# Float64 weights put together by two merges on VectorE, a ScalarE fence in every unit, and a new instruction order, in a fused RWKV attention and channel-mix kernel

## The chip, the cores and the metric

One Trainium2 chip, one of its cores. The metric is the device time of one execution in microseconds (us); several runs of the same kernel are taken and their median is compared.

## What is computed

```python
for t in range(S):                       # S = 768, batch 4, 8 heads, head_dim 48
    kt, vt, rt = k[:, :, t], v[:, :, t], r[:, :, t]
    cur = einsum('bhd,bhe->bhde', u[None] * kt, vt)
    y[:, :, t] = einsum('bhd,bhde->bhe', rt, state + cur)
    state = w[None, :, :, None] * state + einsum('bhd,bhe->bhde', kt, vt)
x = y.transpose(0, 2, 1, 3).reshape(B, S, 384)
x_prev = concatenate([zeros((B, 1, D)), x[:, :-1]], axis=1)
xk = mu_k * x + (1 - mu_k) * x_prev;  xr = mu_r * x + (1 - mu_r) * x_prev
k = maximum(xk @ w_k, 0)                 # w_k 384 x 1024
out = sigmoid(xr @ w_r) * (k * k @ w_v)  # w_r 384 x 384, w_v 1024 x 384
```

The arrays come as float64 where the weights `w_k`, `w_r`, `w_v` are concerned; the kernel gets their 64-bit words and must make float32 numbers of them itself.

## The kernel before, in words

**Attention in units.** The 768 steps are cut into 12 chunks of 64 and the 4 batches into 2 pairs: 24 units. For a unit `u`, `RK{u}` (VectorE) scales the loaded `r` and `k` by decay tables, `Kn{u}` scales `k` for the state, `ru{u}` makes the products for the bonus term. On TensorE, `sc{u}` and `bo{u}` form scores and bonus in PSUM, `Am{u}` (VectorE, two instructions) masks them, `st{u}` multiplies the old state (`from_state`, L565), `va{u}` adds the masked scores times the values (`values`, L586), `up{u}` forms the new state term (`update`, L599). ScalarE then turns the result into the tile `xt` (`tu{u}`, L624), and the state is advanced (`S{u}`; VectorE, and ScalarE for the first two units). PSUM holds one `y` and one `a` at a time, so unit `u + 1` cannot begin `st` before `tu{u}` and `S{u}` have read `y`.

**Single units and blocks.** Units 0 to 4 are single tasks. From unit 5 on, `st`, the scores of the next unit, `va` and `up` are one task `bl{u}`, written out by `block`. Between `from_state` and `values` the array's rows are used in another order, so something must hold `values` back until `from_state` has ended: in single units a fence (a 1x1 copy `tick` on ScalarE that waits for the last matmul of `from_state` and that the first matmul of `values` waits for), in blocks `nc.tensor.drain()`, which waits for all that TensorE has in flight.

**Channel mix in tiles.** Six tiles `m` of 128 steps (four units each), 512 columns. Six mixes per tile (`mixa` and `mixc` on ScalarE, `mixb` and `mixd` on VectorE) give high and low halves; `k{m}.0` to `k{m}.7` are the key products (9 matmuls each: high x high, high x low, low x high, three row blocks), followed on ScalarE by `relu`, `square`, `kh` and on VectorE by `kl`; `r{m}.0` to `.2` are the gates, `v{m}.o.c` the value products (72 matmuls a tile). Tile 0's mixes need the four units 0 to 3 and six small copies `gap0.*` that the SP queue issues after `tu3`.

**Weights.** Ten blocks (4 of `w_k`, 2 of `w_r`, 4 of `w_v`) are loaded as 64-bit words. For each, `shift{b}` (VectorE, L364) moves the high word into place, `rest{b}` (ScalarE, two instructions, L372 and L373) turns two bytes of each word into 16-bit numbers that hold sign and lowest bits together, `merge{b}` (VectorE, L377) joins the two, `hi{b}` (ScalarE) rounds to the high half, and the low half comes from TensorE with ScalarE (`lop`, `loc`, blocks 0 to 3) or from VectorE (`lo{b}`).

**Range test.** The weights are read again, half a block at a time (20 parts, `cw{b}`, two buffers `seen`); ScalarE takes absolute values (`size{b}`, L885), VectorE the largest and the smallest (L888). `check_range` compares them, a matmul `cnt` on TensorE sums the outcome, and a flag chooses at the end between this result and a slow step-by-step version.

**What sets the order.** Each engine runs its instructions strictly in the order in which they are emitted. `Plan.order` emits tasks in a simulated order of time from costs and the lists `ORDER`, one per engine, which cover the time up to the end of tile 0; behind them it goes by the longest tail. `i7` in the TensorE list means seven idle matmuls that keep the clock up. SP issues loads in its list's order, and one that has to wait holds all behind it.

Of the kernel before, what the change touches and what calls it, by code (L numbers as in the profile page):

```python
# [45 lines left out]
LEAST = 1.125 * 2.0 ** -15  # L46
MOST = 3.0e38
# [9 lines left out]
    "PE": """i22 pt sc0 bo0 i9 sc1 bo1 va0 up0 i7 va1 up1 sc2 bo2 i1 st2 lop0.0 va2 up2 lop0.1 i7 st3 sc3 bo3 lop1.1 lop1.0 va3 up3 sc4 bo4 i3 lop2.0  # L57
        lop2.1 st4 i4 va4 up4 lop3.0 sc5 bo5 lop3.1 k0.0.0 k0.0.1 k0.0 k0.1 k0.2 k0.3 bl5 k0.4 k0.5 k0.6 k0.7 bl6 r0.0 r0.1 v0.0.0 v0.0.1 bl7 v0.0.2
        v0.0.3 r0.2 v0.1.0 v0.1.1 v0.1.2 bl8 v0.1.3 v0.2.0 v0.2.1 v0.2.2""",
    "DVE": """tables RK0 ru0 RK1 Am0 ru1 Kn0 Kn1 ru2 RK2 shift0 Am1 merge0 RK3 Kn2 Am2 dec2 dec3 first0 shift1 ru3 Kn3 merge1 S2 shift2 RK4 Am3 merge2 S3  # L60
        shift3 Am4 merge3 mixb0.0.0 RK5 mixd0.0.0 mixb0.0.1 mixb0.0.2 mixd0.0.1 mixd0.0.2 shift4 mixb0.1.0 shift5 merge4 Am5 RK6 S4 merge5 mixd0.1.0
        kl0.0 kl0.1 mixb0.1.1 first1 mixb0.1.2 S5 lo4 kl0.2 RK7 mixd0.1.2 shift6 Am6 mixd0.1.1 kl0.3 lo5 merge6 kl0.4 shift7 kl0.5 merge7 lo6 RK8
        Am7 S6 kl0.7 kl0.6 lo7 shift8 shift9 merge8 RK9 lo8 rs8 Am8 S7 fin0.0 rs9 merge9 mixb1.0.0 mixb1.0.1 lo9 mixd1.0.0 RK10 mixb1.0.2 first2
        mixd1.0.1 Am9""",
    "ACT": """wup wn rest0 S0 tu0 hi0 S1 tu1 tick2 loc0.0 rest1 tu2 hi1 rest2 loc0.1 tick3 loc1.1 tu3 hi2 rest3 omu loc1.0 loc2.0 mixa0.0.0 tick4 hi3
        mixc0.0.0 mixa0.0.1 loc2.1 mixa0.0.2 mixc0.0.1 loc3.0 mixc0.0.2 mixa0.1.0 rest4 loc3.1 rest5 relu0.0 relu0.1 square0.0 tu4 mixa0.1.1
        mixc0.1.0 square0.1 kh0.0 kh0.1 mixa0.1.2 relu0.2 hi4 tu5 square0.2 kh0.2 mixc0.1.2 relu0.3 square0.3 rest6 relu0.4 hi5 kh0.3 mixc0.1.1
        square0.4 rest7 relu0.5 kh0.4 square0.5 kh0.5 relu0.6 hi6 tu6 relu0.7 square0.7 kh0.7 hi7 sg0.0 square0.6 kh0.6 rest8 sg0.1 tu7 rest9 hi8
        mixa1.0.0 mixa1.0.1 hi9 mixc1.0.0 tu8 mixa1.0.2 mixc1.0.1""",
# [21 lines left out]
class Plan:  # L91
# [12 lines left out]
    def add(self, name, engine, cost, call, after=(), lock=False, allocates=(), uses=(), size=0, quads=False, behind=()):  # L104

        assert name not in self.tasks, name
        self.tasks[name] = dict(name=name, engine=engine, cost=cost, call=call, after=[a for a in after if a], lock=lock,
                                allocates=list(allocates), size=size, quads=quads, behind=[b for b in behind if b], n=len(self.tasks))  # L110
# [268 lines left out]

# [746 lines left out]
```

## Time and profile before

| | |
|---|---|
| median of 3 runs | 355.42 us (354.82 to 358.03) |
| profiled execution, whole | 357.5 us |
| its span, first to last instruction | 355.7 us |
| TensorE busy | 327.5 us (92%) |
| VectorE busy | 230.9 us (65%) |
| ScalarE busy | 215.4 us (61%) |
| GpSimd busy | 90.1 us (25%) |
| mean granted TensorE clock | 0.973 |

Busy time is the time in which an engine has an instruction under way. The shares are averages over a start-up of some 50 us, a first tile and five more tiles with different limits, so they have to be read stage by stage. A granted clock of 1.00 is the 2.4 GHz level, 0.50 the 1.2 GHz level.

### The profile page before, as it was taken

What the parts mean: (1) busy time and instruction counts of PE and PEld (TensorE: products, weight loads), DVE (VectorE), ACT (ScalarE), POOL (GpSimd) and SP (SyncE); (2) the same over time, 40 slices, a digit from 0 to 9 for tenths busy, and PEclk for the clock granted to TensorE, in tenths of its full rate; (3) what the DMA queues carried; (4) which work ended last, traced back from release to release, by engine and by line L of the source; (5) the groups of instructions that cost most, each with busy time, mean ns of one, the idle gap of its engine ahead of it and who ended that gap; (6) DMA issues with size and microseconds to landing.
All of it is one profiled execution on the core that took longest, in us unless ns stands there. A gap on an engine that the chain in (4) does not pass through costs nothing. (4 is left out here: it accounts for less than half of the span.)

```text
span 355.7 us, 9895 instructions
## 1 busy us (share of the span) xinstructions
PE 327.5 (92%) x4309; PEld 255.6 (72%) x4309; DVE 230.9 (65%) x346; ACT 215.4 (61%) x327; POOL 90.1 (25%) x86
## 2 busy tenths in 40 slices
PE   8587978979979999999999999999999999999991
PEld 3355655857856778887778877878877778888880
DVE  7845575939689779885897669986766517433000
ACT  2438799999944976365771468662646827288000
POOL 2001504324337043701364403366102200000000
PEclk9878799989999999999999999999999999999998
DMA  7992076623355574616844428625321001100001
GB/s 215 331 328 64 17 229 239 218 82 120 100 135 184 165 227 134 203 55 188 247 143 127 122 76 257 210 69 142 106 95 44 15 5 49 59 2 0 29 35 36
DMA packets 17236, 45.39 MB, mean 128 GB/s; under 512 B 2528, under 2 KB 4704, under 8 KB 17184
## 3 DMA queue, kind: packets, MB, share of 16 engines
q1 hardware_dynamic: 17184, 44.66, 40.8%
q8 instruction: 36, 0.59, 0.7%
q14 instruction: 16, 0.13, 0.1%
HBM read 38.75 MB, written 4.72 MB: 122 GB/s over the span
## 5 line engine op out<-in xcount | busy, mean ns | idle before, releaser
L728 PE MATMUL v<-kh,wv 128*128 128x512 f32 x288 | 92.9, 393 | 0.7 <-ACT wv L413 0.5
L728 PEld LDWEIGHTS v<-kh,wv 128*128 128x128 f32 x288 | 54.0, 188 | 13.3 <-ACT wv L413 0.9
L728 PE MATMUL k<-xh,wk_hi 128*128 128x512 f32 x144 | 58.9, 409 | 3.9 <-ACT kr L760 3.3
L774 DVE TENSOR_TENSOR kl<-kr,kh 128x512 fp32r<-128x512 f32 x48 | 37.8, 790 | 34.6 <-ACT kh L769 34.5
L728 PE MATMUL k<-xl,wk_hi 128*128 128x512 f32 x144 | 57.8, 402 | 0.7 <-DVE xl L749 0.7
L728 PE MATMUL k<-xh,wk_lo 128*128 128x512 f32 x144 | 57.6, 400 | 0.0
L728 PE MATMUL v<-kl,wv 128*128 128x512 f32 x144 | 56.3, 391 | 0.0
L498 POOL TENSOR_TENSOR ru<-tokens,vk 128x384 f32<-128x384 f32 x16 | 20.5, 1281 | 105.3 <-DVE S L615 46.6
L760 ACT ACTIVATE kr<-k 128x512 f32<-128x512 f32 x48 | 28.7, 600 | 23.2 <-PE k L728 22.7
L742 DVE SCALAR_TENSOR_TENSOR xm<-xt,small_sb,xm 128x512 f32<-128x512 f32 x36 | 30.7, 869 | 16.8 <-ACT xm L738 16.1
L738 ACT ACTIVATE xm<-xt,omu 128x512 f32<-128x512 f32 x36 | 25.5, 724 | 21.4 <-DMA xt<-xt 16.2
L513 POOL TENSOR_TENSOR Kn<-vk,wn 128x384 f32<-128x384 f32 x18 | 24.3, 1352 | 52.5 <-DMA vk<-in_vk 27.0
L728 PEld LDWEIGHTS k<-xh,wk_hi 128*128 128x128 f32 x144 | 27.4, 190 | 12.2 <-ACT kr L760 4.2
L728 PEld LDWEIGHTS k<-xl,wk_hi 128*128 128x128 f32 x144 | 27.4, 191 | 7.2 <-DVE xl L749 1.1
L728 PEld LDWEIGHTS k<-xh,wk_lo 128*128 128x128 f32 x144 | 27.5, 191 | 6.7
L765 ACT ACTIVATE kr<-kr 128x512 f32<-128x512 f32 x48 | 30.3, 631 | 1.2
L728 PEld LDWEIGHTS v<-kl,wv 128*128 128x128 f32 x144 | 27.0, 188 | 5.4
L769 ACT CAST kh<-kr 128x512 fp32r<-128x512 f32 x48 | 29.6, 619 | 1.1
L486 DVE TENSOR_TENSOR RK<-rk,table 112x1024 f32<-112x1024 f32 x22 | 29.2, 1329 | 1.3 <-DMA rk<-in_rk 1.3
L797 DVE TENSOR_TENSOR sg<-v,sg 128x512 f32<-128x512 f32 x18 | 12.4, 686 | 25.8 <-PE v L728 21.1
L749 DVE TENSOR_TENSOR xl<-xm,xh 128x512 fp32r<-128x512 f32 x36 | 25.0, 704 | 4.7 <-ACT xh L746 4.1
L746 ACT CAST xh<-xm 128x512 fp32r<-128x512 f32 x36 | 22.3, 620 | 8.9 <-DVE xm L742 8.5
(100 smaller groups left out, 515.1 us busy)
## 6 DMA issues: line engine op xcount, KB each, us to landing
rk<-in_rk SPq DMA_DIRECT2D x22, 448.0 KB, 4.7
vk<-in_vk SPq DMA_DIRECT2D x24, 384.0 KB, 3.7
out<-sg SPq DMA_DIRECT2D x18, 256.0 KB, 2.0
raw_k<-in_wk SPq DMA_DIRECT2D x4, 768.0 KB, 11.5
raw_v<-in_wv SPq DMA_DIRECT2D x4, 768.0 KB, 7.6
tokens<-in_rt SPq DMA_DIRECT2D x16, 192.0 KB, 3.8
seen<-in_wk SPq DMA_DIRECT2D x8, 384.0 KB, 3.6
seen<-in_wv SPq DMA_DIRECT2D x8, 384.0 KB, 4.0
```

Of the source, the lines that this page charges most:

```text
L486: nc.vector.tensor_tensor(out=RK, in0=d["rk"], in1=table[:, :, :, :C], op=ALU.mult)
L498: nc.gpsimd.tensor_tensor(out=ru, in0=late["tokens"][:, u % 2], in1=d["kn"], op=ALU.mult)
L513: engine.tensor_tensor(out=Kn, in0=d["kn"], in1=wn, op=ALU.mult)
L728: nc.tensor.matmul(out=ps, lhsT=a, rhs=x, start=(first and i == 0), stop=(last and i == n - 1))
L738: nc.scalar.mul(out=xm, in_=before, mul=omu[:, j, t:t + 1])
L742: nc.vector.scalar_tensor_tensor(out=xm, in0=now, scalar=mu_sb[:, j, t:t + 1], in1=xm, op0=ALU.mult, op1=ALU.add)
L746: nc.scalar.copy(out=xh, in_=mixed[m, j, t])
L749: nc.vector.tensor_tensor(out=xl, in0=mixed.pop((m, j, t)), in1=xh.bitcast(F32), op=ALU.subtract)
L760: nc.scalar.activation(out=kr, in_=keys[m, f], func=AF.Relu)
L765: nc.scalar.activation(out=kr, in_=kr, func=AF.Square)
L769: nc.scalar.copy(out=kh, in_=keys[m, f])
L774: nc.vector.tensor_tensor(out=kl, in0=kr, in1=kh.bitcast(F32), op=ALU.subtract)
```

## The change

Three of its parts change instructions. `rest` goes: sign and lowest bits are now joined by two VectorE instructions, `w_sign` and `w_low`, each of the form that `w_merge` had. Every unit has the ScalarE fence, blocks included, in place of the drain. The range test's largest and smallest are taken by VectorE straight from the loaded words with an absolute value in the reduction; ScalarE has no part in it; its 20 parts lie in tiles 2 to 5 instead of 1 to 3, and `cnt` goes from `k3.1` to `v5.1.0`. The fourth part is the order: new `ORDER` lists, and other engines for `Kn`, `dec` and `ru` of the first units.

The lists of VectorE up to the first mix of tile 0, before and after:

```
tables RK0 ru0 RK1 Am0 ru1 Kn0 Kn1 ru2 RK2 shift0 Am1 merge0 RK3 Kn2 Am2 dec2 dec3 first0 shift1 ru3 Kn3 merge1 S2 shift2 RK4 Am3 merge2 S3 shift3 Am4 merge3 mixb0.0.0

tables RK0 ru0 Kn0 Am0 RK1 Kn1 RK2 Am1 shift0 sign0 first0 dec2 merge0 Kn2 Am2 dec3 ru3 RK3 shift1 sign1 merge1 S2 Am3 ru4 RK4 S3 shift2 sign2 merge2 Am4 mixb0.0.0
```

The list of SP from `w1` to `w5`, before and after:

```
w1 w2 rk4 vk4 w3 rk5 vk5 gap0.1.0 gap0.0.0 gap0.0.2 gap0.0.1 gap0.1.1 gap0.1.2 w4 w5

w1 w2 rk4 gap0.0.0 gap0.1.0 vk4 gap0.1.1 gap0.0.1 gap0.0.2 gap0.1.2 w3 rk5 vk5 w4 w5
```

`Kn` goes to VectorE for units 0 to 2 and 4 to 7 (before 0 to 3), `dec` for units 2, 3 and 5 to 7 (before 2 and 3), `ru` for units 0 and 3 to 5 (before 0 to 3); GpSimd has the others. The instructions:

```diff
-    def w_rest(b):
...
-        raw = raws[b].bitcast(U8)
-        to = raws[b].bitcast(I16)
-        nc.scalar.activation(out=to[:, :, 0], in_=raw[:, :, 3], func=AF.Identity, scale=1.0 / 32, bias=below[:, 0:1])
-        nc.scalar.activation(out=to[:, :, 1], in_=raw[:, :, 7], func=AF.Identity, scale=-2.0, bias=below[:, 1:2])
-
-    def w_merge(b):
-        a = af[b]
-        nc.vector.scalar_tensor_tensor(out=a, in0=raws[b][:, :, 0], scalar=0x80000007, in1=a,
-                                       op0=ALU.bitwise_and, op1=ALU.bitwise_or)
...
-        add(f"rest{b}", "ACT", 0.1 + 1.3 * n, lambda b=b: w_rest(b), [f"w{b}"], behind=[f"rest{b - 1}" if b else None])
-        add(f"merge{b}", "DVE", 0.07 + 0.8 * n, lambda b=b: w_merge(b), [f"shift{b}", f"rest{b}"], lock=True, uses=[f"raw{b}"])
+        add(f"sign{b}", "DVE", 0.07 + 0.8 * n, lambda b=b: w_sign(b), [f"shift{b}"], lock=True)
+        add(f"merge{b}", "DVE", 0.07 + 0.8 * n, lambda b=b: w_low(b), [f"sign{b}"], lock=True, uses=[f"raw{b}"])
...
-        d["tick"] = nc.scalar.copy(out=tick, in_=ones[:1]) if single(u) else nc.gpsimd.memset(tick, 0.0)
+        d["tick"] = nc.scalar.copy(out=tick, in_=ones[:1])
...
         from_state(u)
+        fence(u)
         if u + 1 < NU:
             scores(u + 1)
             if u + 1 < TOKENS:
                 bonus(u + 1)
-        nc.tensor.drain()
         values(u)
...
-    def sizes(b):
...
-        nc.scalar.activation(out=seen[b], in_=late["seen"][:, b % 2, :n, 1].bitcast(F32), func=AF.Abs)
...
-        nc.vector.tensor_reduce(out=bounds[:, i, b:b + 1], in_=seen[b], op=op, axis=mybir.AxisListType.X)
...
+        nc.vector.tensor_reduce(out=bounds[:, i, b:b + 1], in_=late["seen"][:, b % 2, :n, 1].bitcast(F32), op=op,
+                                axis=mybir.AxisListType.X, apply_absolute_value=True)
...
-        at = (NM - 3) * b // PARTS + 1
+        at = (NM - 2) * b // PARTS + 2
...
-    row.insert(row.index(f"k{NM // 2}.1"), "cnt")
+    row.insert(row.index(f"v{NM - 1}.1.0"), "cnt")
```

The two merges, which only the slow version called until now:

```python
    def w_sign(b):
        a = af[b]
        nc.vector.scalar_tensor_tensor(out=a, in0=raws[b][:, :, 1], scalar=0xC0000000, in1=a,
                                       op0=ALU.bitwise_and, op1=ALU.bitwise_or)

    def w_low(b):
        a = af[b]
        nc.vector.scalar_tensor_tensor(out=a, in0=raws[b][:, :, 0], scalar=29, in1=a,
                                       op0=ALU.logical_shift_right, op1=ALU.bitwise_or)
```

The planner also learns a cost for the fence (`fence=0.5` in a block).

## Rows read from the trace of the kernel before

**Rows 1.** Windows by stage: us, then busy time (instructions) by engine, PEclk, DMA share, GB/s

```profile
0.00:51.30 51.30, 40.57 (x882) 25.58 (x883) 33.32 (x53) 30.64 (x39) 8.31 (x19) 0.87 0.63 195
51.30:111.60 60.30, 53.33 (x749) 41.27 (x747) 44.85 (x63) 53.11 (x67) 22.07 (x16) 0.97 0.51 162
111.60:290.70 179.10, 176.11 (x2407) 142.15 (x2411) 134.94 (x206) 106.27 (x182) 59.71 (x52) 1.00 0.44 132
100.00:110.00 10.00, 8.61 (x156) 6.93 (x156) 9.80 (x14) 4.43 (x7) 5.20 (x5) 1.00 0.68 192
```

**Rows 2.** Timeline of TensorE: the first key product of tile 0 and of tile 1

```profile
51.27 0.39 PE L728 MATMUL k<-xh,wk_hi 128*128 128x512 f32 x1
...
111.60 0.50 PE L728 MATMUL k<-xh,wk_hi 128*128 128x512 f32 x1
```

**Rows 3.** Groups by line and shape, ScalarE: the first conversion of each kind of block

```profile
L372 ACT ACTIVATE raw_v<-raw_v,below 128x768 int16<-128x768 uint8 x4 | 8.2, 2056 | 0.0
...
L372 ACT ACTIVATE raw_k<-raw_k,below 128x768 int16<-128x768 uint8 x4 | 8.1, 2024 | 4.3 <-DMA raw_k<-in_wk 4.3
...
L372 ACT ACTIVATE raw_r<-raw_r,below 128x576 int16<-128x576 uint8 x2 | 3.2, 1610 | 0.0
```

**Rows 4.** Timeline of all engines around unit 2's end and unit 3's start

```profile
29.42 1.99 ACT L373 ACTIVATE raw_k<-raw_k,below 128x768 int16<-128x768 uint8 x1
31.17 0.68 ACT L624 COPY xt<-y 112x512 f32<-112x512 f32 x1
...
32.93 1.13 PE L565 MATMUL y<-RK,S 48*64 48x64 f32 x32 [2.36 <-DVE S L615]
```

**Rows 5.** Groups by line and shape, VectorE: the merges, and Kn where VectorE has it

```profile
L377 DVE SCALAR_TENSOR_TENSOR a_k<-raw_k,a_k 128x768 uint32<-128x768 uint32 x4 | 4.3, 1067 | 6.0 <-ACT raw_k L373 3.6 <-ACT omu L315 2.3
L377 DVE SCALAR_TENSOR_TENSOR a_v<-raw_v,a_v 128x768 uint32<-128x768 uint32 x4 | 4.0, 994 | 1.5 <-ACT raw_v L373 1.5
...
L377 DVE SCALAR_TENSOR_TENSOR a_r<-raw_r,a_r 128x576 uint32<-128x576 uint32 x2 | 1.6, 804 | 1.7 <-ACT raw_r L373 1.7
...
L513 DVE TENSOR_TENSOR Kn<-vk,wn 128x384 f32<-128x384 f32 x4 | 2.1, 550 | 0.0
```

**Rows 6.** Timeline of TensorE: the last part of unit 0's update

```profile
18.23 0.41 PE L599 MATMUL y<-vk,Kn 64*64 64x48 f32 x5 [4.64 <-issue]
```

**Rows 7.** Timeline of the SP queue: the copies gap0

```profile
41.08 4.89 SPq L635 DMA_DIRECT2D xt<-xt  x6
```

**Rows 8.** Timeline of TensorE: one block of a later tile, with its drain

```profile
121.16 0.69 PE L565 MATMUL y<-RK,S 48*64 48x64 f32 x32
121.65 0.67 PE L522 MATMUL a<-RK 48*64 48x64 f32 x32
122.45 0.68 PE L586 MATMUL y<-Am,vk 64*64 64x64 f32 x32
```

**Rows 9.** Timeline: the fences of units 2 and 4

```profile
25.24 0.69 PE L565 MATMUL y<-RK,S 48*64 48x64 f32 x32
...
26.00 0.19 ACT L574 COPY tick<-ones 1x1 f32<-1x1 f32 x1 [1.84 <-PE y L565]
...
47.00 0.17 ACT L574 COPY tick<-ones 1x1 f32<-1x1 f32 x1
...
47.23 0.54 PEld L586 LDWEIGHTS y<-Am,vk 64*64 64x64 f32 x32 [2.45 <-ACT tick L574]
```

**Rows 10.** Timeline of ScalarE: the instruction at a later block's from_state

```profile
162.21 0.60 ACT L760 ACTIVATE kr<-k 128x512 f32<-128x512 f32 x1 [3.13 <-PE k L728]
```

**Rows 11.** Range test: its reductions, its loads; then tile 5's k5.0 and v5.1.0 on TensorE

```profile
L888 DVE TENSOR_REDUCE bounds<-seen 128x1 f32<-128x384 f32 x32 | 16.0, 543 | 1.4 <-ACT seen L885 1.4
...
seen<-in_wv SPq DMA_DIRECT2D x8, 384.0 KB, 4.0
...
308.48 0.39 PE L728 MATMUL k<-xh,wk_hi 128*128 128x512 f32 x1
...
337.10 0.40 PE L728 MATMUL v<-kh,wv 128*128 128x512 f32 x1
```

More of the change, by code (lines that the diff above doesn't have):

```diff
@@ L14 @@
 I32 = mybir.dt.int32
-I16 = mybir.dt.int16
-U8 = mybir.dt.uint8
 AF = mybir.ActivationFunctionType
@@ L46 @@
 LEAST = 1.125 * 2.0 ** -15
+GREATEST = 1.75 * 2.0 ** 16
 MOST = 3.0e38
@@ L56 @@
 ORDER = {
[L57 to L69, printed above, removed]
@@ L70 @@
-    "POOL": """Kn4 ru4 dec4 ru5 Kn5 ru6 dec5 Kn6 Kn7 ru7 dec6 Kn8 ru8 Kn9 dec7 ru9 dec8 ru10""",
-    "SP": """w rk0 vk0 rk1 vk1 rk2 w0 vk2 rk3 vk3 w1 w2 rk4 vk4 w3 rk5 vk5 gap0.1.0 gap0.0.0 gap0.0.2 gap0.0.1 gap0.1.1 gap0.1.2 w4 w5 rk6 vk6 w6 w7 rk7
-        vk7 w8 w9 ut rk8 vk8 rt8 rk9 vk9 gap1.0.0 gap1.1.1 rt9 rt10 gap1.1.0 gap1.1.2 gap1.0.2 gap1.0.1 rk10 rk11 vk10 put0.0 rt11 rk12""",
+    "PE": """i22 pt sc0 bo0 i6 va0 i2 sc1 bo1 up0 sc2 bo2 va1 up1 i5 st2 i2 va2 up2 lop0.0 sc3 bo3 st3 i4 va3 up3 lop0.1 lop1.1 sc4 st4 bo4 i10 va4 i1
+        up4 lop1.0 lop2.1 k0.0.0 lop2.0 k0.0.1 k0.0 k0.1 k0.2 sc5 bo5 k0.3 lop3.0 lop3.1 k0.4 bl5 k0.5 k0.6 k0.7 bl6 r0.0 r0.1 v0.0.0 v0.0.1 v0.0.2
+        bl7 v0.0.3 r0.2 v0.1.0 v0.1.1 v0.1.2 v0.1.3 v0.2.0 bl8 v0.2.1""",
@@ new lines @@
+    "DVE": """tables RK0 ru0 Kn0 Am0 RK1 Kn1 RK2 Am1 shift0 sign0 first0 dec2 merge0 Kn2 Am2 dec3 ru3 RK3 shift1 sign1 merge1 S2 Am3 ru4 RK4 S3 shift2
+        sign2 merge2 Am4 mixb0.0.0 dec5 Kn4 mixd0.0.0 mixb0.0.1 mixb0.0.2 mixd0.0.1 mixd0.0.2 shift3 mixb0.1.0 sign3 ru5 merge3 RK5 kl0.0 shift4 Kn5
+        sign4 mixd0.1.0 kl0.1 merge4 mixb0.1.1 Am5 RK6 S4 shift5 kl0.3 lo4 Kn6 kl0.2 sign5 mixd0.1.1 dec6 shift6 mixb0.1.2 Am6 RK7 S5 kl0.4 merge5
+        sign6 mixd0.1.2 lo5 kl0.5 shift7 merge6 first1 sign7 lo6 merge7 Am7 S6 RK8 Kn7 kl0.7 kl0.6 lo7 shift8 shift9 sign8 sign9 merge8 fin0.0 rs8
+        lo8 merge9 dec7 mixb1.0.0 Am8 S7 RK9 mixb1.0.1 mixd1.0.0 lo9 mixb1.0.2""",
@@ L73 @@
+    "POOL": """ru1 ru2 dec4 Kn3 ru6 ru7 ru8 dec8 Kn8""",
+    "SP": """w rk0 vk0 rk1 vk1 rk2 w0 vk2 rk3 vk3 w1 w2 rk4 gap0.0.0 gap0.1.0 vk4 gap0.1.1 gap0.0.1 gap0.0.2 gap0.1.2 w3 rk5 vk5 w4 w5 rk6 vk6 w6 w7 rk7
+        vk7 w8 w9 ut vk8 rt8 rk8 gap1.0.2 gap1.1.1 gap1.1.0 gap1.0.0 gap1.1.2 rk9 gap1.0.1 rk10 vk9 rk11 put0.0 rt9 rt10 vk10""",
 }
@@ L102, in __init__, with add @@
         self.tasks, self.users, self.bufs = {}, defaultdict(list), {}
-    def add(self, name, engine, cost, call, after=(), lock=False, allocates=(), uses=(), size=0, quads=False, behind=()):
+    def add(self, name, engine, cost, call, after=(), lock=False, allocates=(), uses=(), size=0, quads=False, behind=(), fence=0.0):
         assert name not in self.tasks, name
         self.tasks[name] = dict(name=name, engine=engine, cost=cost, call=call, after=[a for a in after if a], lock=lock,
-                                allocates=list(allocates), size=size, quads=quads, behind=[b for b in behind if b], n=len(self.tasks))
+                                allocates=list(allocates), size=size, quads=quads, behind=[b for b in behind if b], fence=fence, n=len(self.tasks))
         for key in uses:
@@ L176, in order @@
             end = s + t["cost"]
+            if t["fence"]:
+                told = max(s + t["fence"], free["ACT"])
+                free["ACT"] = told + 0.2
+                end = max(end, told + 0.3 + t["cost"] - 2 * t["fence"])
             free[engine] = end
@@ L897, in check_range, with count @@
         n = 2 * NP + PARTS
-        nc.vector.tensor_scalar(out=ok[:, 2 * NP:n], in0=bounds[:, 0], scalar1=2.0, scalar2=None, op0=ALU.is_lt)
+        nc.vector.tensor_scalar(out=ok[:, 2 * NP:n], in0=bounds[:, 0], scalar1=GREATEST, scalar2=None, op0=ALU.is_lt)
         nc.vector.tensor_scalar(out=ok[:, n:], in0=bounds[:, 1], scalar1=LEAST, scalar2=None, op0=ALU.is_ge)
-        cnt = psM.tile([1, ok.shape[1]], F32, tag="m", name="cnt")
+        late["ok"] = ok
+    def count():
+        ok = late["ok"]
+        late["cnt"] = cnt = psM.tile([1, ok.shape[1]], F32, tag="m", name="cnt")
@@ L913, in rwkv_kernel @@
         for i, op in enumerate((ALU.max, ALU.min)):
-            add(f"{op.name}{b}", "DVE", 0.08 + 0.8 * n, lambda b=b, i=i, op=op: bound(b, i, op), [f"size{b}"], lock=True, uses=[f"ca{b}"])
-    add("range", "DVE", 1.5, check_range, [f"max{PARTS - 1}", f"min{PARTS - 1}"], allocates=[("m", "cnt")], uses=["cnt"])
+            add(f"{op.name}{b}", "DVE", 0.08 + 0.8 * n, lambda b=b, i=i, op=op: bound(b, i, op), [f"cw{b}"], uses=[f"seen{b}"])
+    add("range", "DVE", 1.5, check_range, [f"{op}{b}" for op in ("max", "min") for b in range(PARTS)])
@@ L919, in ffn @@
+    add("cnt", "PE", 0.1, count, ["range"], allocates=[("m", "cnt")])
+    add("flag", "DVE", 0.4, decide, ["cnt"], uses=["cnt"])
     def ffn(m):
```

26 lines of the change are left out of this document (13 added, 13 removed).

## The prediction

> **What bounds the kernel now.** I read the windows by stage first [rows 1], then the first key product of tile 0 and of tile 1 in TensorE's timeline [rows 2]. They cut the span into four. Up to 51.3 us no key product runs: attention units 0 to 4 and the first weights are made ready. From 51.3 to 111.6 lies tile 0, in which TensorE has something under way for 53.3 of 60.3 us. From 111.6 on TensorE is busy for 176.1 of 179.1 us in the window shown and goes on so up to about 348.3; a tail of 7.4 us (last output, flag) closes the span of 355.7. The reader is to see that the last five tiles are TensorE's own work: what is done for VectorE or ScalarE there is worth nothing, and only the drains can be taken out. What can be gained lies ahead of 111.6.
>
> There the waiting engine is mostly TensorE and the late one ScalarE: in tile 0 ScalarE is busy 53.1 of 60.3 us [rows 1]. How it holds the chain before that is seen at unit 2 [rows 4]: `tu2` comes at 31.17, right behind the second conversion of a weight block (29.42 + 1.99), and `st3` only at 32.93, released by `S2`, which waits for `tu2`. One conversion is 2.0 us long and there are two a block [rows 3]; the fence of unit 4 was late by the same kind of queue, and TensorE lost 2.45 us to it [rows 9].
>
> **The change part by part.**
>
> *Conversions off ScalarE.* The first instructions of the ten blocks take 8.1 + 3.2 + 8.2 = 19.5 us [rows 3], the second ones are as long: 39 us leave ScalarE, all ahead of 111.6. Of its 30.6 + 53.1 = 83.7 us [rows 1] some 45 stay, so it is no bound there any more. What is late next is VectorE.
>
> *A second merge on VectorE.* The new instruction has the form of the one that is there (same shape, type and stride), so its price is 4.3 + 1.6 + 4.0 = 9.9 us for ten [rows 5]. The new lists also bring VectorE `Kn4` to `Kn7` and `dec5` to `dec7` and take `Kn3` off: net six instructions of 0.55 us, 3.3 us (`dec` has no row of its own here; it is taken as `Kn`). The `ru` that VectorE has stay four. So VectorE's work up to the first key product of tile 1 rises from 33.3 + 44.9 = 78.2 us [rows 1] to about 91. That alone is a bound: 91 us without a single wait, against 111.6 now.
>
> *Start-up.* Unit 0's update stands still from 13.6 to 18.2 for nothing that the profile shows [rows 6], while the loads run; the same loads are issued ahead of it in the new order, so I let it stand. From there to the first key product are 33 us, in which the conversions of blocks 1, 2 and 3 (4 us each) lie in front of `tu2`, of the fence and low halves of unit 3, and of the fence of unit 4: 12 us. They go. In their place the second merges of blocks 0 to 2 stand in VectorE's list ahead of `S2`, `S3` and `Am4`, about 1 us each, part of it beside TensorE's own steps. I take 1 us as left: key products begin at about 40 us instead of 51.3. The copies `gap0` wait for `tu3` in both lists; they go out at 41.08 now [rows 7] and I expect them at about 31. Moved ahead of `vk4`, `w3`, `rk5` and `vk5` in the SP queue, they hold these loads back until then. `w3` serves only key products 6 and 7, and `vk4` unit 4, so I cost this at nothing; the cover is VectorE's own backlog, which reaches `Kn4` and `shift3` some 6 and 10 us after `tu3`. If that cover were gone, a load of 2 to 4 us would show.
>
> *Tile 0.* VectorE sets its end. Through 111.6 it is busy 70% of the time now, 74% within tile 0, and 98% in its fullest window, 100 to 110 [rows 1]. Walking the new list by the durations of the trace, I find waits of about 8 us besides the 91: before the tables, before `wn`, behind unit 0's standstill, and TensorE's last value products behind `lo9`. That is 99 us, a fill of 92%. Tile 1 then begins at 99 instead of 111.6: **-12.6 us**. The ends: no wait at all, 91 us, -20.6; a fill of 84%, 108 us, -3.6.
>
> *The fence for the drain.* In a later block `values` begins 1.29 us after `from_state` (121.16 to 122.45), while the scores in between begin after 0.49 [rows 8]. With the fence, from unit 2: 0.76 us to the tick (25.24 to 26.00) and 0.19 for it; unit 4 shows 0.06 more from the tick's end to TensorE (47.17 to 47.23) [rows 9]: 1.01. So a block gains 0.28 us at best. What queues behind the tick on ScalarE is the relu of the key product just ended: it starts at 162.21 now, 0.1 us after `from_state` [rows 10], and would start some 0.8 us later, which three PSUM tiles of key products cover. What may stand ahead of the tick is the rest of an instruction of 0.6 us, as long as the relu. 15 blocks lie behind 111.6 (units 9 to 23): at best -4.2, at worst for one instruction ahead (+0.3 each) +5; I take 0.2 a block, **-3 us**. The four blocks of tile 0 are inside VectorE's bound.
>
> *Range test.* The 20 ScalarE passes leave an engine that is no bound; the 40 reductions stay, and I take them at today's 0.54 us although they read every second word [rows 11]: nothing, with the cover that TensorE's work gives. A reduction of twice the length would put 22 us more on VectorE over four tiles, where it is busy three quarters of the time; still nothing. The one new place is the end: five parts are loaded after `k5.0`, and `cnt` holds `v5.1.0`. Between them lie 26 us (308.48 + 2.1 to 337.10); three rounds of two buffers at 4.0 us landing and about 2 us of reductions take 18. Nothing, with up to 5 us if VectorE comes to them late.
>
> **The sum:** 357.5 (the profiled execution) - 12.6 - 3 = 341.9. The median of the runs shown is 2.1 us lower than that execution, so 355.4 - 15.6 = **340 us**.
>
> **A rule against a row.** TensorE's standstill at 13.6 to 18.2 [rows 6] counts in this sum as a thing that comes back. The Trainium skill, "Runtime: NRT & Kernel Launch", section "Instruction fetch mechanics", says that instructions are fetched in blocks of 256 and that crossing a block is "mostly hidden". By that rule the standstill is chance, it need not come back, and about 2 us of VectorE's waiting behind it go too: 338 us. The row shows 4.6 us that were not hidden.
>
> **The rivals.**
> *Fuller.* VectorE's list runs almost without waits, or the standstill does not return: tile 1 begins at 91 to 95, and with all of the fence's 4 us the time is 331 to 335. For it: VectorE's 98% window. Against it: the list of before leaves 26% of tile 0 open.
> *Half.* A strict queue with a merge, a mask and a mix in turn waits for ScalarE and TensorE more often than my walk shows: a fill of 84 to 88%, tile 1 at 103 to 108, 344 to 349 us.
> *VectorE's queue as now.* It fills as in tile 0 today, 74%: 91 / 0.74 = 123, tile 1 begins 11 us later than before, and 355.4 + 11 - 3 = 363. The place is VectorE's list up to `lo9`; it decides from a fill of 81% (91 / 111.6) downward. Against it: most of today's waits there are for conversions that are gone (their idle column) [rows 5].
> *The fence late.* In blocks the tick stands behind a whole chain of relu, square and cast, about 1.85 us: 15 x (1.85 - 0.28) = +24, so 366 with the gain of tile 0. It eats that gain from 0.8 us a block. For it: 2.45 us once [rows 9]; against it: ScalarE is only 59% busy in the later tiles [rows 1].
> *The flag.* The test misjudges the words and the slow version runs: many times the time. Both bounds are taken on the same words as before, so hardly.
>
> **How the numbers follow.** Forecast (336 to 344) 0.48; fuller 0.15; half 0.22; no change within 1% (VectorE fill 80 to 83%) 0.06; slower by VectorE's queue 0.05, by the fence 0.03, by the flag 0.01. One per cent, 3.6 us, is about what a measurement here can tell from no change. Faster by more than that: 0.48 + 0.15 + 0.22 = 0.85; same 0.06; slower 0.09. The range leaves out the slower cases, the unchanged one and the ends of half and fuller: 332 to 350.
>
> **What would show it.** First key product near 40 us, tile 1's near 99; ScalarE some 50 us less busy and VectorE some 13 more; VectorE over 88% busy between 20 and 95; `values` about 1.0 us after `from_state` in later blocks, with the wait named ScalarE; no wait at `cnt`; again 4 to 5 us without a cause in unit 0's update. The prediction is wrong if VectorE shows long waits for loads behind `gap0`, if ticks come more than half a microsecond late on the mean, or if `cnt` waits.

## The result and the profile after

The changed kernel takes **341.76 us** in the median of 4 runs (341.01 to 344.5), the one before 355.27 (4 runs): a ratio of 0.9618, 95% interval [0.9544, 0.9692]. The forecast was 340, the range 332 to 350. A later set of 6 runs beside 11 of before gave 340.29 against 357.27, 0.9541 [0.9495, 0.9587]. Medians and ratios leave out runs over 1.5% above the fastest of the same kernel. The profiled execution took 341.01 us, its span 339.3, against 357.5 and 355.7.

Two lines of the page of the changed kernel, busy time of the engines and the granted clock in 40 slices:

```profile
PE 322.2 (95%) x4304; PEld 255.2 (75%) x4308; DVE 238.5 (70%) x362; ACT 173.8 (51%) x306; POOL 90.2 (27%) x78
...
PEclk9959999999979999999999999999999999999998
```

ScalarE lost 41.6 us, VectorE gained 7.6. The clock shows two dips: one in the third slice (17 to 25 us), around TensorE's standstills at the start, and one in the twelfth (93 to 102 us). Both come up again below.

Windows of the changed kernel, by the same columns as [rows 1]:

```profile
0.00:41.60 41.60, 34.70 (x803) 22.41 (x808) 32.98 (x53) 13.58 (x27) 6.15 (x16) 0.88 0.59 186
41.60:100.60 59.00, 56.19 (x822) 44.49 (x821) 56.25 (x80) 35.77 (x64) 24.48 (x10) 0.97 0.63 201
100.60:290.70 190.10, 189.79 (x2503) 155.12 (x2503) 135.09 (x202) 107.85 (x189) 59.54 (x53) 1.00 0.38 118
...
20.00:95.00 75.00, 68.84 (x1258) 52.01 (x1260) 68.33 (x97) 41.28 (x77) 22.97 (x9) 0.96 0.51 163
```

The windows end at the first key products of tiles 0 and 1 (41.67 and 100.64, below). VectorE has changed places with ScalarE: in tile 0 it is busy 56.25 of 59.0 us (before 44.85 of 60.3), ScalarE 35.77 (before 53.11). From 20 to 95 us VectorE is busy 91% of the time. From 100.6 on TensorE has something under way for 189.79 of 190.10 us.

The first key product of each tile in TensorE's timeline cuts the span into stages. The table has this for the kernels of the study (one profiled execution each, us from the span's start), but for the one with both edits of question 3; "VectorE" is its busy time up to tile 1's first key product.

| kernel | tile 0 at | VectorE | tile 1 at | tile 0 | tile 1 | tile 2 | tile 3 | end of matmuls |
|---|---|---|---|---|---|---|---|---|
| before | 51.27 | 78.2 | 111.60 | 60.33 | 48.31 | 49.77 | 50.28 | 348.18 |
| changed kernel | 41.67 | 89.2 | 100.64 | 58.97 | 46.44 | 48.66 | 48.67 | 332.24 |
| the same again | 40.45 | 89.6 | 99.06 | 58.61 | 46.37 | 48.63 | 48.64 | 330.50 |
| before, fence only | 51.47 | | 114.37 | 62.90 | 50.53 | 49.23 | 49.38 | 350.95 |
| changed, drain in all blocks | 42.40 | 88.5 | 98.39 | 55.99 | 47.26 | 49.81 | 49.81 | 333.86 |
| before, merges only | 45.79 | 90.0 | 100.37 | 54.58 | 49.50 | 49.77 | 50.13 | 337.99 |
| changed, order of before | 48.25 | 90.8 | 101.95 | 53.70 | 49.99 | 48.65 | 48.64 | 337.04 |
| changed, six signs twice | 41.30 | 96.1 | 106.87 | 65.57 | 47.93 | 48.67 | 48.68 | 339.98 |
| changed, drain in unit 8 | 41.62 | 88.2 | 97.53 | 55.91 | 49.19 | 48.64 | 48.64 | 331.80 |
| changed, 14 idle matmuls | 42.56 | 89.8 | 100.07 | 57.51 | 47.98 | 48.69 | 48.67 | 333.24 |
| changed, drain up to unit 11 | 43.03 | 87.4 | 98.19 | 55.16 | 47.27 | 48.64 | 48.63 | 330.54 |
| changed, loads first | 43.65 | 89.8 | 100.43 | 56.78 | 47.80 | 48.64 | 48.63 | 333.31 |
| drain up to unit 11, loads first | 42.18 | 87.5 | 96.94 | 54.76 | 47.27 | 48.63 | 48.64 | 329.29 |

Of the 16.4 us by which the span fell, 10.96 came ahead of tile 1, 4.98 in tiles 1 to 5 and 0.46 behind them.

TensorE's timeline of the changed kernel: the updates of units 0 and 1, the first key products, unit 8's block in tile 0, a block of tile 2, and `cnt`:

```profile
13.59 0.64 PE L586 MATMUL y<-vk,Kn 64*64 64x48 f32 x27
16.14 0.40 PE L586 MATMUL y<-vk,Kn 64*64 64x48 f32 x5 [1.91 <-issue]
18.86 1.03 PE L586 MATMUL y<-vk,Kn 64*64 64x48 f32 x26
22.42 0.40 PE L586 MATMUL y<-vk,Kn 64*64 64x48 f32 x6 [2.53 <-issue]
...
41.67 0.39 PE L714 MATMUL k<-xh,wk_hi 128*128 128x512 f32 x1
...
90.77 0.69 PE L552 MATMUL y<-RK,S 48*64 48x64 f32 x32
...
93.80 0.68 PE L573 MATMUL y<-Am,vk 64*64 64x64 f32 x32 [1.40 <-ACT tick L561]
...
100.64 0.39 PE L714 MATMUL k<-xh,wk_hi 128*128 128x512 f32 x1
...
149.27 0.69 PE L552 MATMUL y<-RK,S 48*64 48x64 f32 x32
149.76 0.67 PE L509 MATMUL a<-RK 48*64 48x64 f32 x32
150.28 0.68 PE L573 MATMUL y<-Am,vk 64*64 64x64 f32 x32
...
320.89 0.24 PE L887 MATMUL cnt<-ok,ones 128*1 128x48 f32 x2
```

These answer to [rows 2, 6, 8, 9]. In the block at 149.27 `values` comes 1.01 us after `from_state`, where it was 1.29. In unit 8's block at 90.77 it comes 3.03 us after, and the wait's releaser is the tick. The standstill of unit 0's update is there again; a second one stands in unit 1's. Unit 1's update also ran slower, 26 matmuls in 1.03 us where 27 of unit 0's took 0.64: the granted clock had fallen to 0.50 by then.

VectorE's groups by shape in the changed kernel, the counterparts of [rows 5, 11], two rows of its timeline, and two of the SP queue's (the first copies `gap0`, the load `w3`):

```profile
L388 DVE SCALAR_TENSOR_TENSOR a_v<-raw_v,a_v 128x768 uint32<-128x768 uint32 x4 | 4.6, 1157 | 0.0
...
L383 DVE SCALAR_TENSOR_TENSOR a_k<-raw_k,a_k 128x768 uint32<-128x768 uint32 x4 | 3.8, 956 | 0.1
...
L869 DVE TENSOR_REDUCE bounds<-seen 128x1 f32<-128x384 f32 x32 | 16.1, 543 | 1.6 <-DMA seen<-in_wk 0.9 <-DMA seen<-in_wv 0.4
...
44.41 0.56 DVE L364 TENSOR_SCALAR a_k<-raw_k 128x768 uint32<-128x768 uint32 x1 [1.60 <-DMA raw_k<-in_wk]
...
308.12 0.17 DVE L881 TENSOR_SCALAR ok<-bounds 128x20 f32<-128x20 f32 x1
...
33.32 1.22 SPq L622 DMA_DIRECT2D xt<-xt  x2
...
37.67 0.58 SPq L355 DMA_DIRECT2D raw_k<-in_wk  x1
```

The merges no longer wait (idle 0.0 and 0.1 us, before 6.0 and 1.5). The reductions take 543 ns as before. `shift3` waited 1.60 us for the load `w3`.

### The profile page after: what moved, and what is told of

It reads as the page before. It is cut to its first block, busy times and chain, and to the rows that moved or that the text cites. A ratio compares the mean times of both kernels' runs of the same rounds, so it can differ in the third digit from the quotient of the medians.

```text
span 339.3 us, 9858 instructions
## 1 busy us (share of the span) xinstructions
PE 322.2 (95%) x4304; PEld 255.2 (75%) x4308; DVE 238.5 (70%) x362; ACT 173.8 (51%) x306; POOL 90.2 (27%) x78
## 5 line engine op out<-in xcount | busy, mean ns | idle before, releaser
L714 PE MATMUL v<-kh,wv 128*128 128x512 f32 x288 | 93.9, 397 | 0.3 <-DVE wv L404 0.3
L714 PE MATMUL k<-xh,wk_hi 128*128 128x512 f32 x144 | 58.2, 404 | 0.0
L714 PE MATMUL k<-xl,wk_hi 128*128 128x512 f32 x144 | 57.0, 396 | 0.0
L760 DVE TENSOR_TENSOR kl<-kr,kh 128x512 fp32r<-128x512 f32 x48 | 36.9, 772 | 13.6 <-ACT kh L755 13.6
L593 POOL TENSOR_TENSOR dec<-S,table 112x384 f32<-112x384 f32 x15 | 24.0, 1602 | 53.9 <-DVE S L602 53.9
L485 POOL TENSOR_TENSOR ru<-tokens,vk 128x384 f32<-128x384 f32 x16 | 17.9, 1120 | 74.9 <-DMA vk<-in_vk 19.1
L732 ACT CAST xh<-xm 128x512 fp32r<-128x512 f32 x36 | 22.4, 621 | 13.6 <-DVE xm L728 13.3
L473 DVE TENSOR_TENSOR RK<-rk,table 112x1024 f32<-112x1024 f32 x22 | 26.6, 1211 | 0.4 <-DMA rk<-in_rk 0.4
```

The source lines that it names most:

```text
L473: nc.vector.tensor_tensor(out=RK, in0=d["rk"], in1=table[:, :, :, :C], op=ALU.mult)
L485: nc.gpsimd.tensor_tensor(out=ru, in0=late["tokens"][:, u % 2], in1=d["kn"], op=ALU.mult)
L593: engine.tensor_tensor(out=dec, in0=S_t[q][:, :, :, :D], in1=decay, op=ALU.mult)
L714: nc.tensor.matmul(out=ps, lhsT=a, rhs=x, start=(first and i == 0), stop=(last and i == n - 1))
L732: nc.scalar.copy(out=xh, in_=mixed[m, j, t])
L760: nc.vector.tensor_tensor(out=kl, in0=kr, in1=kh.bitcast(F32), op=ALU.subtract)
```

## The experiments

**1. Which part carries the gain.** Four kernels shared their runs of before (357.13 us, 12 runs). The first is before with the fence alone:

```diff
-        d["tick"] = nc.scalar.copy(out=tick, in_=ones[:1]) if single(u) else nc.gpsimd.memset(tick, 0.0)
+        d["tick"] = nc.scalar.copy(out=tick, in_=ones[:1])
...
         from_state(u)
+        fence(u)
...
-        nc.tensor.drain()
         values(u)
```

> The kernel before with nothing changed but the drain of the blocks, which becomes the fence on ScalarE. If a fence in time is worth 0.28 us, the 15 blocks behind tile 0 give -4.2 us, and the four of tile 0, where ScalarE is 88% busy with conversions, 0 to +4: 351 to 355 us. If the tick stands behind a chain of instructions as a rule, 10 us or more are added: 365 or later.

Measured: 358.36 us, ratio 1.0034 [1.0003, 1.0065], above the range expected. In TensorE's timeline of this kernel stands unit 6's `values`, in ScalarE's its tick:

```profile
79.63 1.12 PE L586 MATMUL y<-Am,vk 64*64 64x64 f32 x32 [2.22 <-ACT tick L574]
...
77.57 1.99 ACT L373 ACTIVATE raw_v<-raw_v,below 128x768 int16<-128x768 uint8 x1
79.31 0.25 ACT L574 COPY tick<-ones 1x1 f32<-1x1 f32 x1
```

The tick stood behind a conversion of 1.99 us. Four of the blocks in tile 0 waited 0.36, 2.22, 1.55 and 1.83 us for their ticks, and tile 1 began 2.8 us later than in before. Tiles 2 to 4 then took 2.2 us less, but tile 1, in which unit 9's tick was 1.56 us late, took 2.2 more. Beside the conversions the fence gains nothing.

The second is the change without the fence:

```diff
         from_state(u)
-        fence(u)
...
+        nc.tensor.drain()
         values(u)
```

> The changed kernel with the drain back in the blocks. The changed kernel gained 5.3 us behind the first key product of tile 1. If that is the fence, 4.2 us come back, less some 1.5 because unit 8's tick came late and its drain would not: 344 to 346 us. If the later tiles gained because the range test left ScalarE, the drain costs under 1 us: 342 to 343.

Measured: 341.94 us, 0.9535 [0.9472, 0.9598], the same as the changed kernel within what can be told, and below both ranges expected. The table says why: tile 0 begins 0.73 us later and takes 2.98 less, so tile 1 begins 2.25 earlier, and tiles 1 to 4 take 3.87 more (195.40 against 191.53). The fence gave 3.87 / 15 = 0.26 us a block behind tile 0, and cost 2.25 us of tile 1's start.

The third has the merges alone, in the lists of before (a `sign` is put behind each `shift` in VectorE's; that edit is left out here):

```diff
-        add(f"rest{b}", "ACT", 0.1 + 1.3 * n, lambda b=b: w_rest(b), ...
-        add(f"merge{b}", "DVE", 0.07 + 0.8 * n, lambda b=b: w_merge(b), ...
+        add(f"sign{b}", "DVE", 0.07 + 0.8 * n, lambda b=b: w_sign(b), [f"shift{b}"], lock=True)
+        add(f"merge{b}", "DVE", 0.07 + 0.8 * n, lambda b=b: w_low(b), [f"sign{b}"], lock=True, uses=[f"raw{b}"])
```

> The kernel before with its own order, drain, engines and range test; only the two conversions are gone and a sign merge stands behind each shift. If the conversions on ScalarE held the start-up and tile 0, this alone brings the first key product of tile 1 from 111.6 to 101 to 106: 345 to 350 us. If the new order carries the gain (old lists that were made around the conversions hold VectorE up), 352 to 357.

Measured: 347.62 us, 0.9735 [0.9663, 0.9806]. Tile 1 begins at 100.37, as in the changed kernel. Windows of it up to the first key products of tiles 0 and 1:

```profile
0.00:45.80 45.80, 36.49 (x882) 23.15 (x883) 38.07 (x57) 15.48 (x30) 9.65 (x19) 0.96 0.67 209
45.80:100.40 54.60, 51.72 (x749) 42.27 (x749) 51.88 (x70) 32.32 (x55) 22.48 (x16) 0.97 0.58 185
```

VectorE: 38.07 + 51.88 = 90.0 of 100.4 us. Key products begin 4.1 us later than in the changed kernel and tile 1 at the same time. The merges alone thus give all of the gain ahead of tile 1.

The fourth is the changed kernel in the order of before (its `ORDER`, left out here, with each `sign` behind its `shift`):

```diff
-KN = ["DVE", "DVE", "DVE", "POOL", "DVE", "DVE", "DVE", "DVE", "POOL", ...
+KN = ["DVE"] * 4 + ["POOL"] * 20
...
+DEC = ["DVE"] * 4 + ["POOL"] * 20
...
+RU = ["DVE"] * 4 + ["POOL"] * 20
```

> The changed kernel's instructions (merges, fence, range test) in the order and on the engines of the kernel before, the sign merge right behind each shift. If the order is worth little, 341 to 346 us. If the order carries most of the gain, 348 to 353, with VectorE waiting in its list before 100 us.

Measured: 346.14 us, 0.9666 [0.9595, 0.9737]. Windows of it, up to tile 1 and in its first matmuls, and a row of TensorE's timeline from there:

```profile
0.00:48.20 48.20, 40.30 (x881) 25.09 (x882) 37.72 (x56) 15.44 (x30) 9.56 (x17) 0.89 0.69 196
48.20:101.90 53.70, 49.98 (x749) 40.76 (x748) 53.05 (x70) 33.02 (x59) 24.57 (x16) 1.00 0.58 190
...
104.40:106.90 2.50, 1.34 (x4) 1.11 (x5) 2.31 (x4) 1.30 (x3) 0.55 (x1) 0.83 0.56 210
106.90:109.40 2.50, 2.50 (x7) 1.93 (x7) 2.20 (x4) 2.09 (x4) 0.00 (x0) 0.50 0.00 0
...
105.56 0.50 PE L715 MATMUL k<-xl,wk_hi 128*128 128x512 f32 x1 [1.81 <-DVE xl L736]
```

Without the new order the key products begin 6.6 us later, tile 1 only 1.3. The other 3.55 us of the order's worth lie inside tile 1: at 103.7 TensorE waited 1.81 us for a low half `xl` of tile 1's mix on VectorE, its busy time was 1.34 of 2.50 us, and the granted clock went to 0.83 and then to 0.50. Tile 1 is not the same in every kernel with the new order either (46.4 to 49.2 us), so one execution does not settle the size.

Together: of 13.5 to 17 us the merges alone give 9.5 (357.13 to 347.62). The order is worth 0.5 to 1.3% by the ratios (0.9666 without it, 0.9618 and 0.9541 with it; the intervals of the first two overlap), 2 to 4.5 us. Fence and range test, the difference between the third and the fourth kernel, come to 1.5 us, which their intervals leave open.

**2. Does VectorE set the start of tile 1?** Four kernels beside 356.83 us for before (11 runs) belong here and to question 3. The first repeats one instruction of the six blocks 4 to 9; the second `or` changes nothing in the words:

```diff
-        ... lambda b=b: w_sign(b), [f"shift{b}"], lock=True)
+        ... lambda b=b: [w_sign(b) for _ in range(2 if b >= 4 else 1)], [f"shift{b}"], lock=True)
```

> The changed kernel with the sign merge of blocks 4 to 9 done twice (the second time it changes nothing): 4 x 0.87 + 2 x 0.66 = 4.8 us more on VectorE in tile 0. If VectorE sets the end of tile 0, tile 1 begins 3.5 to 5 us later: 345 to 347 us. If TensorE or a load sets it, the addition is hidden: 342 to 343.

Measured: 349.0 us, 0.979 [0.9756, 0.9824]. Windows of it up to the first key products of tiles 0 and 1:

```profile
0.00:41.30 41.30, 35.24 (x807) 22.34 (x808) 33.03 (x53) 13.64 (x27) 6.16 (x16) 0.88 0.62 188
41.30:106.80 65.50, 58.07 (x821) 45.14 (x821) 63.06 (x85) 35.82 (x64) 17.43 (x8) 0.95 0.55 176
```

VectorE's busy time up to tile 1 rose from 89.2 to 96.1 us, tile 1 went from 100.64 to 106.87. VectorE's share, 90%, is about that of the changed kernel (89%). Work that is put on VectorE ahead of tile 1 is paid nearly one for one. Busy time rose by 6.9 us and not by the 4.8 expected, and the time lies above the range: two of the sign merges took 2.46 and 1.72 us where the others took 0.95 and 0.75, and both ran while GpSimd had an instruction under way.

**3. The late tick of unit 8, and the standstill.** In the changed kernel's ScalarE timeline the tick of 93.58 stands behind two instructions of tile 1's mixes, the first of which had waited for VectorE:

```profile
92.35 0.62 ACT L732 CAST xh<-xm 128x512 fp32r<-128x512 f32 x1 [2.25 <-DVE xm L728]
92.95 0.72 ACT L724 ACTIVATE xm<-xt,omu 128x512 f32<-128x512 f32 x1
93.58 0.17 ACT L561 COPY tick<-ones 1x1 f32<-1x1 f32 x1
```

Its windows around that place show what the granted clock did:

```profile
90.00:95.00 5.00, 3.36 (x132) 2.69 (x130) 5.00 (x7) 1.50 (x4) 4.00 (x1) 0.95 0.45 137
95.00:97.50 2.50, 2.50 (x10) 1.93 (x8) 2.50 (x5) 2.22 (x4) 0.28 (x1) 0.50 0.90 243
97.50:100.00 2.50, 2.50 (x12) 2.02 (x11) 2.06 (x4) 1.13 (x2) 2.42 (x2) 0.91 0.91 281
```

TensorE was busy 3.36 of 5.00 us, and then the clock was 0.50 for 2.5 us and 0.91 for 2.5: 1.25 + 0.22 = 1.5 us of its time lost, besides the wait of 1.40. The second execution of the same kernel has a wait of 1.41 us there and 0.52 and 0.80 in the windows behind it. In the kernel with the drain in all blocks the same stretch runs at 1.00:

```profile
95.00:97.50 2.50, 2.50 (x13) 2.04 (x12) 2.50 (x4) 1.58 (x3) 0.24 (x1) 1.00 0.98 295
```

The fall does not follow from the wait alone. In the kernel of question 4 with the loads first, the same tick is as late and the clock stays at 1.00:

```profile
95.11 0.68 PE L573 MATMUL y<-Am,vk 64*64 64x64 f32 x32 [1.41 <-ACT tick L561]
...
95.00:97.50 2.50, 2.39 (x70) 2.10 (x71) 2.50 (x4) 1.23 (x4) 0.95 (x1) 1.00 0.91 277
```

The traces of the kernels in the table hold 28 waits of TensorE of over 1 us between 40 and 330 us; behind 10 of them the clock fell to about 0.50. What decides was not tried.

The kernel tried has the drain in unit 8's block alone:

```diff
-        fence(u)
+        if u != 8:
+            fence(u)
...
+        if u == 8:
+            nc.tensor.drain()
```

> The changed kernel with the drain in unit 8 alone, whose tick waited on ScalarE behind a mix (values 3.0 us after from_state). If that wait is on the path, 1.7 us are won: 340 us. If VectorE's last weight merges and mixes set the start of tile 1 all the same, 0 to 0.5: 341.5.

Measured: 340.78 us, 0.9575 [0.9534, 0.9615]. Tile 1 began at 97.53, but it took 49.19 us instead of 46.44: unit 9's tick was now the late one, by 2.65 us. It stood behind a queue of relus, squares and casts that had built up behind a cast that waited 3.03 us for VectorE's mix. The lateness had only moved one block on:

```profile
109.85 0.68 PE L573 MATMUL y<-Am,vk 64*64 64x64 f32 x32 [2.65 <-ACT tick L561]
```

The other two kernels take eight of the 22 idle matmuls ahead of unit 0 away, the second with the drain in unit 8 as well:

```diff
-    "PE": """i22 pt sc0 bo0 i6 va0 ...
+    "PE": """i14 pt sc0 bo0 i6 va0 ...
```

> The changed kernel with 14 idle matmuls at the start in place of 22, so 16 TensorE instructions fewer lie ahead of everything. If TensorE's standstills in the updates of units 0 and 1 are waits for the next part of its program, they come 16 instructions later in the program, behind the two updates; VectorE's waits for S1 (3.0 us) and for wn (1.8 us) shrink, and the time falls by 2 to 4 us: 338 to 340. If they are waits for a load, they stay in the updates at the same time, 16.1 and 22.4, and the time falls by 0 to 1.

> Both together. If both are on the path one after the other, 336 to 338 us; if the same queue of VectorE hides one behind the other, no better than the better of the two.

Measured: 341.48 us, 0.9574 [0.9541, 0.9606], and 339.5 us, 0.9514 [0.9481, 0.9548]. The intervals of these two and of the last one meet, so no gain of one over the other is shown. TensorE's timeline with `i14`:

```profile
12.86 0.68 PE L586 MATMUL y<-vk,Kn 64*64 64x48 f32 x32
...
22.53 1.44 PE L248 MATMUL idle_ps<-idle 128*128 128x512 bf16 x3 [2.11 <-issue]
```

Unit 0's update now runs whole, behind it TensorE waits 1.98 us for VectorE's mask. The second standstill lies among the idle matmuls behind unit 1's update: it went to a later instruction. That it ends at 22.53, near the 22.42 of the changed kernel, says little, since the second execution of the changed kernel ended it at 21.35.

What does not change is the count. In every trace of the study that has them, the first and the second standstill come behind 448 to 450 and 704 to 706 instructions of TensorE (matmuls and weight loads; a few records are missing), 256 apart, whatever the instruction is. And the page's table of DMA queues has one of the kind `instruction` that brings 16 KB at a time. In the changed kernel such a transfer ended at 14.62 and one at 21.01, and TensorE went on at 16.14 and 22.42. In the fourteen traces 27 standstills of over 0.35 us without a named wait stand at these counts or seven times 256 further on, and every one ended 1.3 to 1.8 us after such a transfer. So they are waits for the next part of TensorE's program, as the first half of the expectation has it; what makes that part late was not tried.

The time did not fall with it. The two kernels with 14 idle matmuls have one more standstill, the one seven times 256 instructions further on (1.68 us, up to 70.69, in the first of them), and its clock is 0.54 from 73.5 to 76. VectorE gained nothing at the start: its wait for unit 0's state went, and one of 3.52 us for `tu2` at 28.58 took its place.

**4. A fence that is late nowhere, and the loads ahead of the copies.** Four kernels beside 357.27 us for before (11 runs): the changed one again (340.29, above), the drain in blocks 5 to 11 with the fence behind them, the loads `vk4` and `w3` ahead of `gap0`, and both.

> The changed kernel, unaltered, on the same chip as the three below: 341 to 342 us, the measure for them.

```diff
-        fence(u)
+        if u >= 12:
+            fence(u)
...
+        if u < 12:
+            nc.tensor.drain()
```

> The changed kernel with the drain in units 5 to 11 and the fence from unit 12 on. If the fence loses in the first two tiles (ticks behind mixes that wait for VectorE, and the clock that falls with it) what it gains later, the second tile ends as with drains everywhere, 1.4 us sooner, and the later tiles stay at 48.7 us each: 1.4 to 2 us less than the changed kernel. If a lost wait only moves to the next place, 0 to 0.5 less.

```diff
-    ... rk4 gap0.0.0 gap0.1.0 vk4 gap0.1.1 gap0.0.1 gap0.0.2 gap0.1.2 w3 rk5 vk5 ...
+    ... rk4 vk4 w3 gap0.0.0 gap0.1.0 gap0.1.1 gap0.0.1 gap0.0.2 gap0.1.2 rk5 vk5 ...
```

> The changed kernel with the loads vk4 and w3 ahead of the copies gap0 in the SP list. VectorE waited 1.6 us for w3 at the start of tile 0. If VectorE's list sets the end of tile 0, these 1.6 us come off: 1 to 2 us less. If they are regained further on in any case, no change; if the loads now hold up TensorE's program at unit 2, 1 to 3 us more, with the standstill longer than today's 2.5.

> Both together. If they act at different places, 2.5 to 3.5 us less than the changed kernel; if one hides the other, no better than the better of the two.

Measured: early drain 339.49 us, 0.9496 [0.9453, 0.9539]; loads first 340.58, 0.9535 [0.9488, 0.9582]; both 339.49, 0.9511 [0.9471, 0.9552]. Windows of the early drain:

```profile
0.00:43.00 43.00, 35.36 (x803) 23.02 (x808) 33.10 (x53) 13.61 (x27) 6.17 (x16) 0.84 0.59 181
43.00:98.20 55.20, 54.36 (x823) 43.63 (x822) 54.26 (x77) 34.62 (x58) 17.91 (x7) 1.00 0.65 202
```

By the stages both gains are there: tile 0 takes 55.16 us at a clock of 1.00 (with the fence 58.61 in the same set), tile 2 48.64 (with the drain 49.81). But key products began at 43.03 instead of 40.45, and the median is 0.8 us below the changed kernel's with intervals that overlap. It has the lowest ratio of all after the change, and that is not a shown gain over the changed kernel. What holds over several kernels is the start of tile 1: 98.39, 97.53, 98.19 and 96.94 where unit 8 has the drain, 100.64, 99.06 and 100.43 where its tick is late.

With the loads first VectorE's wait for `w3` is gone, but no time is won. Two rows of TensorE and `shift3` on VectorE, in that kernel:

```profile
16.22 0.40 PE L586 MATMUL y<-vk,Kn 64*64 64x48 f32 x5 [2.27 <-issue]
...
23.05 0.40 PE L586 MATMUL y<-vk,Kn 64*64 64x48 f32 x6 [3.09 <-issue]
...
44.68 0.56 DVE L364 TENSOR_SCALAR a_k<-raw_k 128x768 uint32<-128x768 uint32 x1
```

`shift3` runs at 44.68 without a wait (44.41 with one). The standstills were 2.27 and 3.09 us, 5.36 together, against 4.44 in the changed kernel and 5.34 in its second execution, and key products began at 43.65. Among kernels that differ in nothing ahead of it, this start lay between 40.45 and 43.03, and with the early drain and the loads first it was 42.18. What the moved loads cost or give is not settled at the size of 1 to 2 us.

## Why the prediction was right, point by point

**VectorE sets tile 0's end: right.** Its work up to tile 1 was put at 91 us and measured at 89.2; the fill at 92%, and measured 89 to 90% in all eleven executions of the table that have the two merges. Doubling six instructions moved tile 1 by 6.2 us. That the order moves the first key product by 6.6 us and tile 1 by 1.3 says the same: an earlier start of key products there gains little. Tile 1 was expected at 99 and came at 100.64 in the profiled execution, 99.06 in the second.

**Start-up: right in size.** 40 us expected, 41.67 and 40.45 measured. The rival of VectorE's queue as now (74%) is excluded, and a fill of 84 to 88%, as *Half* had it, was not seen either. *Fuller* was not reached: the earliest tile 1 of the study begins at 96.94, not at 91 to 95. *The fence late* happened to single blocks and not as a rule: of the 19 blocks of the changed kernel, TensorE waited for the tick in two, 1.40 us in unit 8 and 0.31 in unit 23.

**The fence: the mechanism right, two terms mis-sized.** In later blocks -3 us was taken for 15 blocks, with -4.2 as the best; the drain kernel shows -3.9. The step that failed is "The four blocks of tile 0 are inside VectorE's bound": they cost 2.25 us of tile 1's start. The prediction named a reason only for later tiles, the tick behind a chain on ScalarE. At unit 8 ScalarE stands waiting for VectorE's mix in its strict order and the tick stands behind that wait, so VectorE's lateness reaches TensorE twice; and in two of the three executions with this late tick (changed kernel twice, loads first) the clock fell behind it. The net worth of the fence is thus 1.6 us by the profiled executions and nothing that can be told by the ratios (0.9535 with the drain, 0.9618 and 0.9541 with the fence), not 3.

That the sum still came out is in part luck. The span fell by 16.4 us where 15.6 were forecast: ahead of tile 1 1.64 us were missing (10.96 of 12.6), and behind it 5.44 came instead of 3. Of these the fence gave 3.87, and 1.05 were gained in tile 1 that no term had (48.31 before, 47.26 with the drain). The order of tile 1's first mixes is the likely place of these, as the run in the old order, with its wait at 103.7, lost 3.55 us there; it was not tried alone. The prediction also read 2.45 us as lost by TensorE at unit 4's fence; the row is that of the weight loads, and the matmuls behind them waited 1.96.

**The moved loads: the price of nothing was short.** VectorE waited 1.60 us for `w3` (the row at 44.41). The cover was as long as named: VectorE came to `shift3` at 42.81, 9.5 us after the first copy went out at 33.32 (31 expected). But `w3`, behind all six copies, was issued only at 37.67, and `shift3` could begin 6.7 us later. Whether this reached the end is open, as said.

**The range test at nothing: right.** Its last comparison ran at 308.12, `cnt` at 320.89 with no wait of TensorE: 12 us of margin. It was not moved alone.

**The standstill came back: right in size, in two places.** Expected were 4 to 5 us in unit 0's update; measured were 1.91 us there and 2.53 in unit 1's, 4.44 together, and 1.65 + 3.69 in the second execution. The Trainium skill, "Runtime: NRT & Kernel Launch", section "Instruction fetch mechanics", has it that crossing a block of instructions is "mostly hidden"; the rows of both kernels show several microseconds that were not. That "it need not come back", as that rule would have it, is excluded: the standstills are waits for the next part of the program, as the count and the instruction transfers of question 3 show.

**ScalarE 50 us less, VectorE 13 more: 41.6 and 7.6.** The 19 added ticks took 3.7 us of ScalarE, which the prediction did not count there. On VectorE the second merges and the moved operations came in about as priced (+9.0 for the merges, +3.4 for `Kn` and `dec`), but `RK` fell from 1329 to 1211 ns a piece and gave 2.6 us back. The rest is a matter of counting: the prediction adds durations, and busy time counts instructions that overlap once (by the sum of durations ScalarE lost 46.3 us and VectorE gained 9.9). The mean of `RK` fell because three of its 22 instructions in before took 2.04 to 2.10 us, each while GpSimd was at work, and none in the changed kernel took over 1.23. Rows of before (the group, then one of the three and the GpSimd instruction beside it):

```profile
L486 DVE TENSOR_TENSOR RK<-rk,table 112x1024 f32<-112x1024 f32 x22 | 29.2, 1329 | 1.3 <-DMA rk<-in_rk 1.3
...
83.92 2.04 DVE L486 TENSOR_TENSOR RK<-rk,table 112x1024 f32<-112x1024 f32 x1
...
83.71 1.17 POOL L513 TENSOR_TENSOR Kn<-vk,wn 128x384 f32<-128x384 f32 x1 [10.66 <-DMA vk<-in_vk]
```

## What to carry to other kernels

Here VectorE was busy 89 to 90% of the time up to tile 1 in every kernel with the two merges, whatever the order, so the sum of its work told the start of tile 1 to a few per cent; an earlier start of other engines then showed little. Look for such an engine, and price a change by what it adds there. A fence that is a small instruction on another engine is as cheap as that engine's queue is short at that moment: count it per block where the queue runs free, and ask in the full stage what stands ahead of it and whom that waits for. A short stall of TensorE can have a second price in the granted clock behind it, and had it behind 10 of 28 waits here, so look at the windows that follow a wait as well as at the wait. And when an engine stands still without a named wait, count its instructions up to there in several kernels, and look at the instruction queue, before guessing at a cause.

## What the hardware showed that was not expected

- A wait of TensorE of 1.40 us was followed by 2.5 us at a clock of 0.50 and 2.5 us at 0.91, during which it was busy all the time; in the kernel with the old order a wait of 1.81 us by 0.83 and 0.50. Behind a wait of 1.41 us at the same place (loads first) and one of 2.65 us (drain in unit 8) the clock stayed at 1.00.
- TensorE's standstills at the start came 256 instructions apart, at the same count in all programs, and each ended 1.3 to 1.8 us after a 16 KB transfer of the instruction queue. They were up to 4.9 us long while loads ran (309 GB/s from 16.0 to 22.4 us of the changed kernel); with one exception, seven times 256 further on in two kernels, later places of that spacing show none.
- A reduction that takes the absolute value and reads every second word took 543 ns for 384 elements, as long as the plain one from packed words.
- VectorE's instructions ran long only beside GpSimd. In the fourteen traces 222 of them took at least 0.4 us and 40% longer than the shortest of their form, and every one of these overlapped an instruction of GpSimd; the `RK` multiply, 1.2 us else, took 2.04 us beside one. Some 100 others in each trace overlapped one as well and did not run long; what makes the difference was not tried.
